# Declaring operations in different banks of one three-bank PSUM tile independent

## The chip, the cores and the metric

The kernel runs on one core of a Trainium2 chip. The metric is the device time of one execution in microseconds. Engines are named as in the profile: PE is TensorE (PEld its weight loads), DVE is VectorE, ACT is ScalarE, POOL is GpSimd, and SP is SyncE, whose queue starts most DMAs.

## The reference

Two layers in a row, all in float32. The first is attention that keeps, per query, the 32 largest scores; the second mixes channels of its output, with each row's predecessor mixed in.

```python
# q, k, v: (8, 8, 576, 64); d_model 512, d_ff 1024
scores = 1/sqrt(64) * q @ k.T
kth = the 32nd largest score of each row
attn = softmax(where(scores >= kth, scores, -1e9))
x = (attn @ v), heads laid side by side: (8, 576, 512)

x_prev = x shifted down by one row (a zero row first)
xk = mu_k * x + (1 - mu_k) * x_prev
xr = mu_r * x + (1 - mu_r) * x_prev
k = maximum(xk @ w_k, 0)
out = sigmoid(xr @ w_r) * ((k * k) @ w_v)
```

## The kernel before, in words

**Tiles of work.** Attention goes by visits: one batch, one pair of heads, and half of the query rows. A visit has four or five tiles of 128 x 576 scores. Tiles 0 to 7 of a head pair come in twos: tile i (even) belongs to the one head and tile i+1 to the other. Tile 8 holds the last 64 rows of both heads. For a pair of tiles the steps are these, with their engine and the line that the profile shows:

- *score* (PE, L890): two matmuls of 64 x 512, one for each head, one into bank 0 and one into bank 2 of the PSUM tile `ps`; the profile counts four, as a float32 matmul is done in two passes here. For tile 8 it is *score8* (L875, L877).
- *sliver* (PE, L885): the last 64 keys of both heads, into bank 1.
- *keep* (ACT, L895), twice: copies 576 scores to `sc`. For the first head they are columns 0 to 575 of `ps` (banks 0 and 1), for the second columns 960 to 1535 (banks 1 and 2).
- DVE, ACT and POOL then find the 32 largest (`cand` L900, `top` L902 and L923, `sg` L920 and L922), ACT takes exponentials (`se`, L928), and DVE masks them into `E` (L931).
- *turn* (PE, L937) transposes the first 512 columns of `E`, and ACT copies them to `et` (L939).
- *turnl* (PE, L946) transposes the last 64 columns of both heads into columns 832 to 959 of `ps` (bank 1), and ACT copies them to `el` (L948).
- *weigh* (PE, L969 and L971): the sums over values, from `et`, `el` and `v`, into columns 576 to 831 of `ps` (bank 1). It is in bank 1 like the data that `el` is copied from, so it follows that copy.
- *place* (DVE, L1005 for two pairs, L1008 for a single one): multiplies the sums by the inverse row sums and writes them to `xT`.

The second layer runs in chunks of 256 rows on `rot` tiles, which are separate PSUM tiles; its matmuls are L607 to L609. The weights are split into two parts at the start (L1174 to L1191).

**Order.** All operations are entered in a graph (`plan.op`) with a cost, a key and the buffers that they read and write. `Plan.run` then works out, engine by engine, an order with planned start times. In this plan a PSUM buffer has a list of banks, and an operation waits for other engines' operations in the same banks only. The operations are then issued in the planned order, and the program is built with that order as it stands (`tc.manual_schedule()`).

**Waits.** The kernel writes no semaphores. The framework that builds the program adds them, from the tiles that instructions share. `ps` is a single tile of three banks for it, and the planner's buffers are slices of it:

```python
a = pp.tile([128, 3 * 512], F32, name="ps")
made["psA"], made["psB"], made["sl"] = ([a[:, :512]], [(0,)], False), ([a[:, 1024:]], [(2,)], False), ([a], [(1,)], False)
made["sums0"], made["sums1"] = ([a[:, 576:704]], [(1,)], False), ([a[:, 704:832]], [(1,)], False)
made["last"] = [a[:, 832:960]], [(1,)], False
```

The second part of each entry is the planner's list of banks. Score has `psA` and `psB`, so banks 0 and 2. Sliver, turnl, `el`, weigh and place have bank 1. Keep has 0 and 1, or 1 and 2. Score8 has 0 and 1.

Of the kernel before, what the change touches and what calls it, by code (L numbers as in the profile page):

```python
# [13 lines left out]
AF = mybir.ActivationFunctionType  # L14
# [3 lines left out]
B, H, S, D = 8, 8, 576, 64  # L18
# [4 lines left out]
MAIN = 512  # L23
REST = S - MAIN
NKC = MAIN // 128
# [4 lines left out]
SCALE = 1.0 / math.sqrt(D)  # L30
BELOW = 1.0 - 2.0 ** -24
# [12 lines left out]
           w=13.895, wabs=-2.072, wclamp=0.971, wshift=-11.985, wsign=1.043, wexp=-1.834, wfine=-0.159, whi=3.263, wmul=9.248, wsub=-9.325, wlo=1.928,  # L44
# [16 lines left out]
LAST, JOINT, PEAT = "last", True, 112  # L61
LWAT, LWSTEP = 1.027, 1.455
LAG0, LAG1 = 10.828, 1.959
WPE = 12
MORE = dict(xh=2, xl=2, et=3, top=3, el=1)


class Buf:
    __slots__ = ("kind", "turn", "slot", "left", "users", "wrote", "read")
# [29 lines left out]


class Op:
    __slots__ = ("lane", "cost", "lat", "f", "base", "key", "pace", "mode", "bufs", "deps", "need", "then", "at", "end", "name", "n")


class Clock:
# [213 lines left out]
def planned(graph):  # L319
    return graph().run()[0]  # L320
# [3 lines left out]
def topk_attention_channel_mix(ctx: ExitStack, tc: tile.TileContext, q, k, v, mu_k, mu_r, w_k, w_v, w_r, out):  # L324
    nc = tc.nc
# [5 lines left out]
    ident = consts.tile([128, 128], F32, name="ident")  # L331
# [3 lines left out]
    ranks_i = consts.tile([128, 9], I32, name="ranks_i")  # L335
# [439 lines left out]
    def attend(plan, visits, X, pair_sums):  # L775
# [8 lines left out]
        for p, (b, hp, part) in enumerate(visits):  # L784
            P = Env()
# [71 lines left out]
            for i in part:  # L857
                n = at0 + i - P.first
                T = Env()
                T.i, T.P = i, P  # L860
                j, u = i % 2, i // 2 % 2
                if i % 4 == 0 or i == P.first:
                    U = Env()
# [3 lines left out]
                if i % 2 == 0:  # L867
                    E, el = buf("E"), buf("el")
                T.sc, T.cand, T.top = buf("sc"), buf("cand"), buf("top")
                if i == 8:  # L870
                    ps, sl = [buf("psA")], buf("sl")

                    def score8(P=P, ps=ps, sl=sl):
                        qd = P.kd.t[:, 128:]
                        nc.tensor.matmul(ps[0].t, lhsT=qd, rhs=P.K.t, start=True, stop=True)  # L875
                        for h in range(2):
                            nc.tensor.matmul(sl.t[:, MAIN:S], lhsT=qd, rhs=P.kd.t[:, h * 64:(h + 1) * 64], start=h == 0, stop=h == 1)  # L877
                    plan.op(PE_, "score8", n, 1190, 1380, score8, reads=[P.K, P.kd], writes=[*ps, sl], mode="Z")
                elif j == 0:
                    ps, sl = [buf("psA"), buf("psB")], buf("sl")  # L880
                    c = (i - P.first) // 2

                    def sliver(P=P, sl=sl, c=c):
                        to = sl.t[:, 512:1408].rearrange("p (h x) -> p h x", h=2)[:, :, :64]
                        nc.tensor.matmul(to, lhsT=P.qs.t[:, c * 128:(c + 1) * 128], rhs=P.kd.t[:, :128].rearrange("p (h x) -> p h x", h=2), start=True, stop=True)  # L885

                    def score(P=P, ps=ps, c=c):
                        for h in range(2):
                            w = slice(h * 64, (h + 1) * 64)
                            nc.tensor.matmul(ps[h].t, lhsT=P.qs.t[w, c * 128:(c + 1) * 128], rhs=P.K.t[w], start=True, stop=True)  # L890
                    plan.op(PE_, "score", n, 965, 1155, score, reads=[P.K, P.qs], writes=ps, mode="S")
                    plan.op(PE_, "sliver", n, 230, 420, sliver, reads=[P.kd, P.qs], writes=[sl], mode="T")

                def keep(T=T, x=ps[j] if i < 8 else ps[0], sl=sl, o=960 if j else 0):
                    nc.scalar.activation(T.sc.t, sl.t[:, o:o + S], AF.Copy)  # L895
                plan.op(ACT, "keep", n, 530, 648, keep, reads=[ps[j] if i < 8 else ps[0], sl], writes=[T.sc])
                for c in range(NCH):
                    w = CUTS[c + 1] - CUTS[c]
# [42 lines left out]
                if i % 2 or i == 8:  # L941
                    es = [T] if i == 8 else [tiles[i - 1], T]
                    pl = buf(LAST)

                    def turn_l(E=E, pl=pl, o=448 if i == 8 else 512):
                        nc.tensor.transpose(pl.t[:, :128], E.t[:, o:o + 128], ident)  # L946
                    plan.op(PE_, "turnl", n, 109, 300, turn_l, reads=[(E, jj) for jj in range(len(es))], writes=[pl, (el, "held")], mode="T")
                    plan.op(ACT, "el", n, 157, 285, lambda el=el, pl=pl: nc.scalar.activation(el.t, pl.t[:, :128], AF.Copy), reads=[pl], writes=[el])  # L948
                    u = (i - U.i) // 2
                    if u == 0:  # L950
                        U.pa = [buf(x) for x in ("sums0", "sums1")[:(U.w + 1) // 2]]

                    def weigh(U=U, P=P, es=es, el=el, u=u, i=i):
                        hs = [slice(j * 64, (j + 1) * 64) for j in range(2)]
                        if i < 8:
                            pa = U.pa[u].t
                            vs = [P.v.t[:, j] for j in range(2)]
                            vr = P.vr.t
                            ms = [[t.et.t[:, c * 128:(c + 1) * 128] for t in es] for c in range(NKC)]
                            ls = [el.t] * 2  # L960
                        else:
                            pa = U.pa[0].t[:, :64]
                            vs = [P.v.t[:, j] for j in range(2)]
                            vr = P.vr8.t
                            ms = [[es[0].et.t[:, c * 128 + j * 64:c * 128 + (j + 1) * 64] for j in range(2)] for c in range(NKC)]
                            ls = [el.t[:, h] for h in hs]
                        for c in range(NKC):
                            for j in range(2):
                                nc.tensor.matmul(pa[hs[j]], lhsT=vs[j][:, c, :], rhs=ms[c][j], start=(c == 0), stop=False)  # L969
                        for j in range(2):  # L970
                            nc.tensor.matmul(pa[hs[j]], lhsT=vr[:, j], rhs=ls[j], start=False, stop=True)  # L971
                    cost = 1140 if i < 8 else 629
                    plan.op(PE_, "weigh", n, cost, cost + 197, weigh, reads=[t.et for t in es] + [el] + [P.v, P.vr if i < 8 else P.vr8], writes=[U.pa[u]], mode="W")
                if i % 4 == 3 or i == part[-1]:
                    U.ri, pr = buf("ri"), buf("rot")
                    w, m = U.w, (U.w + 1) // 2
# [22 lines left out]
                    cost = 206 if i == 8 else 50 + 107 * m  # L999
                    plan.op(ACT, "ri", n, cost, cost + 117, out_ri, reads=[pr], writes=[U.ri])  # L1000

                    def place(U=U, x=xT[b], hp=hp, i=i, m=m):
                        to = x.t[:, hp, 1 + U.i * 64:1 + min(S, U.i * 64 + m * 128)]
                        if m == 2:
                            nc.vector.tensor_mul(to.rearrange("p (u q) -> p u q", u=2), pair_sums, U.ri.t.rearrange("p (u q) -> p u q", u=2))  # L1005
                        else:
                            n = 64 if i == 8 else 128
                            nc.vector.tensor_mul(to, U.pa[0].t[:, :n], U.ri.t[:, :n])  # L1008
                    cost = 130 if i == 8 else 64 + 136 * m
                    plan.op(DVE, "place", n, cost, cost + 90, place, reads=[*U.pa, U.ri], writes=[(xT[b], (hp, U.i // 2 + u)) for u in range(m)], after=X.late if b == 1 else ())  # L1010
                    for u in range(m):
# [1 line left out]
            if hp == HP - 1:  # L1013
                o = slice(part[0], part[-1] + 1)
# [181 lines left out]
    def pipeline(stack):  # L1196
        one = stack.enter_context(tc.tile_pool(name="one", bufs=1))
# [8 lines left out]
        made = {}  # L1206
# [14 lines left out]
        c = pp.tile([128, 2 * 512], F32, name="se")  # L1221
# [4 lines left out]
        pair_sums = a[:, 576:832].rearrange("p (u q) -> p u q", u=2)  # L1226
# [7 lines left out]
        def graph():  # L1234
            plan = Plan()
            for name, (tiles, banks, free) in made.items():
                plan.kind(name, len(tiles), banks, free)
                plan.kinds[name].tiles = tiles
            X = Env()
            X.ranks, X.least, X.mu = plan.buf("ranks"), plan.buf("least"), plan.buf("wmu")  # L1240
            def consts_in():
                nc.vector.tensor_copy(X.ranks.t[:, :9], ranks_i)
                if JOINT:
                    nc.vector.memset(X.ranks.t[:, 9:10], -SCALE)
                    nc.vector.memset(X.ranks.t[:, 10:11], BELOW)
            plan.op("DVE", "ranks", -9, 250, 350, consts_in, writes=[X.ranks])
            plan.op("SP", "mu", 1.0, 1100, 2900, load_mu, writes=[X.mu])
            plan.op("DVE", "nmu", 3.0, 80, 183, lambda: nc.vector.tensor_scalar(nmu, mu, -1.0, 1.0, op0=OP.mult, op1=OP.add), writes=[X.mu])
            weights(plan, X)
            mixes(plan, *attend(plan, VISITS, X, pair_sums), X)  # L1250
            return plan

        for o in planned(graph):
            o.f()

    with ExitStack() as stack:
        stack.enter_context(tc.manual_schedule())
# [12 lines left out]
    with tc.If(again > 0):  # L1270
        with tc.For_i(0, B, 1) as b, ExitStack() as stack:
# [8 lines left out]
            for hp in range(HP):  # L1280
                P = Env()
                P.hp = hp
                prep_all(g, P, lambda x: x[bass.ds(b, 1)].rearrange("o h s d -> (o h) s d"), hp, L)
                for i in range(9):
                    T = Tile_()
# [51 lines left out]
```

## Time and profile before

| | |
|---|---|
| median of 3 runs | 1324.69 us (1323.78 to 1325.32) |
| profiled execution, its own time | 1327.52 us |
| its span, from the first instruction to the last | 1325.7 us |
| PE busy | 1237.7 us (93%) |
| DVE busy | 1152.2 us (87%) |
| ACT busy | 1133.4 us (85%) |
| POOL busy | 985.9 us (74%) |
| mean granted PE clock | 0.988 |

The busy times are sums over a run whose first 60 us load and split weights and whose last 130 us have the second layer alone, so a share in the middle is higher than here. In lists of groups, "idle before" is the time that an engine sat idle just ahead of these instructions, with the instruction that ended the wait. Matmuls overlap by some 0.06 us, and their ends are modelled.

### The profile page before, as it was taken

The page shows a single profiled execution, that of the slowest core. Times are in us where ns is not written, and L with a number is a line of the kernel's source. Part 1 is how long each engine was busy: PE and PEld are TensorE (multiplying, and loading weights), DVE is VectorE, ACT ScalarE, POOL GpSimd, SP SyncE. Part 2 cuts the span into 40 slices and gives each one's busy share as a digit, 9 for nine tenths or more (in the row PEclk, how much of TensorE's full clock was granted, in tenths as well). Part 3 has the DMA queues.
Part 4 walks back from the last instruction along what each step waited for, and adds up shares of the span by engine and source line. Part 5 has one row for each costly group of instructions (what it writes and reads, how often), then busy time and mean ns, then how long its engine had stood idle before and what let it go on. Part 6 is the DMA issues. An engine that isn't in the chain of part 4 may idle for free.

```text
span 1325.7 us, 31110 instructions
## 1 busy us (share of the span) xinstructions
PE 1237.7 (93%) x9349; PEld 940.2 (71%) x9349; DVE 1152.2 (87%) x6228; ACT 1133.4 (85%) x2491; POOL 985.9 (74%) x885
## 2 busy tenths in 40 slices
PE   5877899999999999999999999999999999999996
PEld 2434667777677776777777777787777777777885
DVE  6999999999999998999999999999898999997211
ACT  5897899999998998899999999998989899988441
POOL 2457997878678685877779687786878788778682
PEclk9997999999999999999999999999999999999998
DMA  7143212221221212122221222212221222221100
GB/s 204 39 108 95 55 43 63 47 62 24 55 64 45 57 34 66 35 62 47 62 47 34 54 55 54 51 37 63 46 62 31 58 47 61 45 54 40 40 24 15
DMA packets 218593, 72.51 MB, mean 55 GB/s; under 512 B 211248, under 2 KB 211248, under 8 KB 218416
## 3 DMA queue, kind: packets, MB, share of 16 engines
q1 hardware_dynamic: 217872, 70.31, 21.6%
q8 instruction: 76, 1.25, 0.4%
q14 instruction: 101, 0.83, 0.2%
q10 hardware_dynamic: 544, 0.13, 0.0%
HBM read 60.95 MB, written 9.44 MB: 53 GB/s over the span
## 4 chain that ended last, share of the span: by engine, by line
PE 57%; ACT 20%; DVE 14%; POOL 3%; issue 3%; DMA 1%; SPq 1%; ACTq 0%; DVEq 0%; POOLq 0%
PE rot L607 9%; PE rot L609 8%; PE rot L608 8%; PE ps L890 8%; PE ps L969 7%; PE rot L937 6%; ACT sg L920 4%; ACT sc L895 4%; DVE cand L900 3%; ACT et L939 3%; ACT se L928 3%; DVE E L931 2%; PE ps L885 2%; DVE top L923 2%; PE rot L833 2%
## 5 line engine op out<-in xcount | busy, mean ns | idle before, releaser
L922 POOL TENSOR_TENSOR sg<-sc,sg 128x576 f32<-128x576 f32 x288 | 408.4, 1421 | 191.5 <-ACT sg L920 189.7
L900 DVE MAX8 cand<-sc 128x8 f32<-128x82 f32 (+1 forms) x2016 | 377.2, 231 | 23.7 <-ACT sc L895 21.8
L920 ACT ACTIVATE sg<-sc,seen 128x576 f32<-128x576 f32 x288 | 225.4, 783 | 14.2 <-DVE seen L912 12.7
L931 DVE SCALAR_TENSOR_TENSOR E<-sc,seen,se 128x576 f32<-128x576 f32 x288 | 231.0, 802 | 0.8 <-PE ps L946 0.2
L923 DVE MAX8 top<-sg 128x8 f32<-128x576 f32 x288 | 215.9, 750 | 11.6 <-POOL sg L922 10.6
L928 ACT ACTIVATE se<-sc,seen 128x576 f32<-128x576 f32 x288 | 216.8, 753 | 8.1 <-DVE E L931 6.3
L895 ACT ACTIVATE sc<-ps 128x576 f32<-128x576 f32 x288 | 186.5, 654 | 28.4 <-DVE E L931 10.2
L937 PE MATMUL rot<-ident,E 128*128 128x128 f32 x1152 | 180.9, 281 | 15.7 <-DVE E L931 7.2
L969 PEld LDWEIGHTS ps<-et,v 128*64 128x64 f32 x2560 | 130.9, 138 | 77.1 <-ACT el L948 46.7
L969 PE MATMUL ps<-et,v 128*64 128x128 f32 (+1 forms) x2560 | 169.5, 271 | 15.9 <-ACT el L948 13.7
L902 DVE MAX8 top<-cand 128x8 f32<-128x56 f32 x864 | 179.1, 208 | 3.7
L607 PE MATMUL rot<-xh,wk 128*128 128x256 f32 (+2 forms) x608 | 180.6, 297 | 1.3 <-ACT ri L998 0.5
L939 ACT ACTIVATE et<-rot 128x512 f32<-128x512 f32 x288 | 173.3, 603 | 7.5 <-PE rot L937 7.2
L937 PEld LDWEIGHTS rot<-ident,E 128*128 128x128 f32 x1152 | 130.0, 141 | 68.6 <-issue 11.4
L608 PE MATMUL rot<-xl,wk 128*128 128x256 f32 (+2 forms) x608 | 170.1, 280 | 0.9 <-POOL xl L1092 0.9
L609 PE MATMUL rot<-xh,wk 128*128 128x256 f32 (+2 forms) x608 | 169.9, 279 | 0.0
L890 PE MATMUL ps<-K,qs 64*128 64x512 f32 x512 | 148.3, 657 | 2.2 <-ACT el L948 1.5
L607 PE MATMUL rot<-wv,hh 128*128 128x512 f32 (+1 forms) x296 | 127.2, 430 | 0.4 <-ACT qs L838 0.3
L607 PEld LDWEIGHTS rot<-xh,wk 128*128 128x128 f32 x608 | 116.4, 191 | 5.2 <-ACT qs L838 1.5
L609 PE MATMUL rot<-wv,hl 128*128 128x512 f32 (+1 forms) x296 | 116.9, 395 | 0.0
L608 PEld LDWEIGHTS rot<-xl,wk 128*128 128x128 f32 x608 | 115.9, 191 | 1.1 <-POOL xl L1092 1.1
L608 PE MATMUL rot<-wv,hh 128*128 128x512 f32 (+1 forms) x296 | 115.9, 392 | 0.0
(113 smaller groups left out, 2834.6 us busy)
## 6 DMA issues: line engine op xcount, KB each, us to landing
kn<-in_k SPq DMA_DIRECT2D x136, 128.0 KB, 2.5
v<-in_v SPq DMA_DIRECT2D x136, 128.0 KB, 2.5
out<-eb SPq DMA_DIRECT2D x35, 256.0 KB, 2.2
qn<-in_q SPq DMA_DIRECT2D x126, 64.0 KB, 2.2
stage<-in_moe_w_k SPq DMA_DIRECT2D x8, 512.0 KB, 6.3
xT<-in_moe_w_v SPq DMA_DIRECT2D x8, 512.0 KB, 3.6
tl<-in_k SPq DMA_DIRECT2D x136, 16.0 KB, 2.0
vr_in<-in_v SPq DMA_DIRECT2D x128, 16.0 KB, 2.1
```

The costliest lines, as they stand in the source:

```text
L607: nc.tensor.matmul(ps, lhsT=sh, rhs=mh, start=first, stop=False)
L608: nc.tensor.matmul(ps, lhsT=sh, rhs=ml, start=False, stop=False)
L609: nc.tensor.matmul(ps, lhsT=sl, rhs=mh, start=False, stop=last)
L890: nc.tensor.matmul(ps[h].t, lhsT=P.qs.t[w, c * 128:(c + 1) * 128], rhs=P.K.t[w], start=True, stop=True)
L900: lambda T=T, c=c: nc.vector.max(T.cand.t[:, 8 * c:8 * c + 8], T.sc.t[:, CUTS[c]:CUTS[c + 1]]), reads=[T.sc], writes=[(T.cand, c)])
L920: lambda T=T, sn=sn: nc.scalar.activation(T.side.t, T.sc.t, AF.Sign, bias=sn(T, 1), scale=-BELOW, accum_out=T.top.t[:, TOPK:TOPK + 1]),
L922: plan.op(POOL, "below", n, 1375, 1430, lambda T=T: nc.gpsimd.tensor_mul(T.side.t, T.sc.t, T.side.t), reads=[T.sc], writes=[T.side])
L923: plan.op(DVE, "eighth", n, 660, 754, lambda T=T: nc.vector.max(T.top.t[:, 24:32], T.side.t), reads=[T.side], writes=[(T.top, 3)])
L928: plan.op(ACT, "exps", n, 667, 754, lambda T=T, pe=pe, sn=sn: nc.scalar.activation(pe.t, T.sc.t, AF.Exp, bias=sn(T, 0), scale=SCALE), read ...
L931: lambda T=T, U=U, pe=pe, sn=sn: nc.vector.scalar_tensor_tensor(T.e(), T.sc.t, sn(T, 2), pe.t, op0=OP.is_ge, op1=OP.mult, accum_out=U.rs.t ...
L937: nc.tensor.transpose(pt.t[:, c * 128:(c + 1) * 128], E.t[:, o + c * 128:o + (c + 1) * 128], ident)
L969: nc.tensor.matmul(pa[hs[j]], lhsT=vs[j][:, c, :], rhs=ms[c][j], start=(c == 0), stop=False)
```

## The change

The functions that issue operations now return their instructions. After each operation is issued, in the planned order, its banks are looked up. If all of them are among 0, 1 and 2, which are those of `ps`, the operation is compared with the last 16 such operations. Where the other one is of another engine, has no bank in common with it and no buffer slot in common with it, every instruction of the one is declared free of a dependency on every instruction of the other. Order, tiles and operations are the same.

```diff
+LOOK = 16
...
 class Op:
-    __slots__ = (..., "name", "n")
+    __slots__ = (..., "name", "n", "made")
...
                     def score(P=P, ps=ps, c=c):
-                        for h in range(2):
-                            w = slice(h * 64, (h + 1) * 64)
-                            nc.tensor.matmul(ps[h].t, lhsT=P.qs.t[w, c * 128:(c + 1) * 128], rhs=P.K.t[w], start=True, stop=True)
+                        ws = [slice(h * 64, (h + 1) * 64) for h in range(2)]
+                        return [nc.tensor.matmul(ps[h].t, lhsT=P.qs.t[w, c * 128:(c + 1) * 128], rhs=P.K.t[w], start=True, stop=True) for h, w in enumerate(ws)]
...
+        past = []
         for o in planned(graph):
-            o.f()
+            got = o.f()
+            banks = {k for b in o.bufs for k in b.kind.banks[b.slot]}
+            if banks and banks <= {0, 1, 2}:
+                o.made = [x.ins for x in (got if isinstance(got, list) else [got])]
+                slots = {(b.kind, b.slot) for b in o.bufs}
+                for p, bs, ss in past:
+                    if p.lane != o.lane and not bs & banks and not ss & slots:
+                        for x in o.made:
+                            for y in p.made:
+                                tc.declare_no_dep(x, y, reason="other banks of one tile")
+                past = [*past, (o, banks, slots)][-LOOK:]
```

The other functions that write or read `ps` (score8, sliver, keep, turn_l, weigh, place) get the same `return`.

More of the change, by code (lines that the diff above doesn't have):

```diff
@@ L101 @@
 class Op:
-    __slots__ = ("lane", "cost", "lat", "f", "base", "key", "pace", "mode", "bufs", "deps", "need", "then", "at", "end", "name", "n")
+    __slots__ = ("lane", "cost", "lat", "f", "base", "key", "pace", "mode", "bufs", "deps", "need", "then", "at", "end", "name", "n", "made")
 class Clock:
@@ L874, in score8 @@
                         qd = P.kd.t[:, 128:]
-                        nc.tensor.matmul(ps[0].t, lhsT=qd, rhs=P.K.t, start=True, stop=True)
-                        for h in range(2):
-                            nc.tensor.matmul(sl.t[:, MAIN:S], lhsT=qd, rhs=P.kd.t[:, h * 64:(h + 1) * 64], start=h == 0, stop=h == 1)
+                        return [nc.tensor.matmul(ps[0].t, lhsT=qd, rhs=P.K.t, start=True, stop=True),
+                                *[nc.tensor.matmul(sl.t[:, MAIN:S], lhsT=qd, rhs=P.kd.t[:, h * 64:(h + 1) * 64], start=h == 0, stop=h == 1) for h in range(2)]]
                     plan.op(PE_, "score8", n, 1190, 1380, score8, reads=[P.K, P.kd], writes=[*ps, sl], mode="Z")
@@ L884, in sliver @@
                         to = sl.t[:, 512:1408].rearrange("p (h x) -> p h x", h=2)[:, :, :64]
-                        nc.tensor.matmul(to, lhsT=P.qs.t[:, c * 128:(c + 1) * 128], rhs=P.kd.t[:, :128].rearrange("p (h x) -> p h x", h=2), start=True, stop=True)
+                        return nc.tensor.matmul(to, lhsT=P.qs.t[:, c * 128:(c + 1) * 128], rhs=P.kd.t[:, :128].rearrange("p (h x) -> p h x", h=2), start=True, stop=True)
                     def score(P=P, ps=ps, c=c):
-                        for h in range(2):
-                            w = slice(h * 64, (h + 1) * 64)
-                            nc.tensor.matmul(ps[h].t, lhsT=P.qs.t[w, c * 128:(c + 1) * 128], rhs=P.K.t[w], start=True, stop=True)
+                        ws = [slice(h * 64, (h + 1) * 64) for h in range(2)]
+                        return [nc.tensor.matmul(ps[h].t, lhsT=P.qs.t[w, c * 128:(c + 1) * 128], rhs=P.K.t[w], start=True, stop=True) for h, w in enumerate(ws)]
                     plan.op(PE_, "score", n, 965, 1155, score, reads=[P.K, P.qs], writes=ps, mode="S")
@@ L894, in keep @@
                 def keep(T=T, x=ps[j] if i < 8 else ps[0], sl=sl, o=960 if j else 0):
-                    nc.scalar.activation(T.sc.t, sl.t[:, o:o + S], AF.Copy)
+                    return nc.scalar.activation(T.sc.t, sl.t[:, o:o + S], AF.Copy)
                 plan.op(ACT, "keep", n, 530, 648, keep, reads=[ps[j] if i < 8 else ps[0], sl], writes=[T.sc])
@@ L945, in turn_l @@
                     def turn_l(E=E, pl=pl, o=448 if i == 8 else 512):
-                        nc.tensor.transpose(pl.t[:, :128], E.t[:, o:o + 128], ident)
+                        return nc.tensor.transpose(pl.t[:, :128], E.t[:, o:o + 128], ident)
                     plan.op(PE_, "turnl", n, 109, 300, turn_l, reads=[(E, jj) for jj in range(len(es))], writes=[pl, (el, "held")], mode="T")
@@ L966, in weigh @@
                             ls = [el.t[:, h] for h in hs]
[L967 to L971, printed above, removed]
+                        return [*[nc.tensor.matmul(pa[hs[j]], lhsT=vs[j][:, c, :], rhs=ms[c][j], start=(c == 0), stop=False) for c in range(NKC) for j in range(2)],
+                                *[nc.tensor.matmul(pa[hs[j]], lhsT=vr[:, j], rhs=ls[j], start=False, stop=True) for j in range(2)]]
                     cost = 1140 if i < 8 else 629
@@ L1004, in place @@
                         if m == 2:
[L1005 to L1008, printed above, removed]
+                            return nc.vector.tensor_mul(to.rearrange("p (u q) -> p u q", u=2), pair_sums, U.ri.t.rearrange("p (u q) -> p u q", u=2))
+                        n = 64 if i == 8 else 128
+                        return nc.vector.tensor_mul(to, U.pa[0].t[:, :n], U.ri.t[:, :n])
                     cost = 130 if i == 8 else 64 + 136 * m
@@ L1241, in consts_in @@
             def consts_in():
[L1242 to L1245, printed above, removed]
+                return [nc.vector.tensor_copy(X.ranks.t[:, :9], ranks_i), nc.vector.memset(X.ranks.t[:, 9:10], -SCALE), nc.vector.memset(X.ranks.t[:, 10:11], BELOW)]
             plan.op("DVE", "ranks", -9, 250, 350, consts_in, writes=[X.ranks])
```

## The prediction

> **What bounds the kernel now.** I read the page first: span, busy times and the chain that ended last.
> ```profile
> span 1325.7 us, 31110 instructions
> PE 1237.7 (93%) x9349; PEld 940.2 (71%) x9349; DVE 1152.2 (87%) x6228; ACT 1133.4 (85%) x2491; POOL 985.9 (74%) x885
> PE 57%; ACT 20%; DVE 14%; POOL 3%; issue 3%; DMA 1%; SPq 1%; ACTq 0%; DVEq 0%; POOLq 0%
> ```
> No engine is the bound by itself: TensorE (PE) carries 57% of the chain, and the chain crosses over to ScalarE (ACT) and VectorE (DVE) for another third. So I split the body of the run, 60 to 1195 us, with the view of busy time by stretch (columns: stretch, its length, busy time of PE, PEld, DVE, ACT, POOL, then granted clock, DMA).
> ```profile
> 60.00:400.00 340.00, 304.81 (x2322) 224.56 (x2321) 324.86 (x1742) 307.58 (x674) 263.18 (x231) 0.97 0.24 61
> 400.00:700.00 300.00, 288.32 (x2253) 219.76 (x2252) 279.79 (x1570) 270.60 (x603) 228.16 (x202) 1.00 0.21 50
> 700.00:1195.00 495.00, 484.91 (x3814) 377.04 (x3812) 463.17 (x2574) 451.96 (x1001) 389.61 (x346) 1.00 0.21 51
> ```
> Up to 400 us DVE is the tight engine: 15.1 us idle against 35.2 on PE. From 400 us on it is PE: 11.7 and 10.1 us idle, against 20.2 and 31.8 on DVE.
>
> Next I asked for the waits of PE over the whole run, and for the copy `el` (L948), which the list puts first. In the answer for L948, the lines before the "who waited for it" pair say what ended ACT's idle time ahead of it (us, times); the last two say who sat idle for it.
> ```profile
> PE ps L969 <- ACT el L948: 13.7, 36, 0.4
> PE ps L885 <- ACT sc L895: 7.4, 16, 1.0
> PE rot L937 <- DVE E L931: 7.2, 6, 3.2
> ```
> ```profile
> L948 ACT ACTIVATE el<-ps x160: 253/277/326, 37.6 to 1239.3; 128x128 f32<-128x128 f32 x160
>   PE ps L890: 37.2, 51
>   PE ps L946: 7.4, 12
>   PEld ps L969: 46.7, 49
>   PE ps L969: 13.7, 36
> ```
> `el` copies what the transpose L946 wrote in bank 1. Yet in 51 of its 160 runs ACT stood idle for it, 37.2 us in all, until the **score** matmuls L890 had ended, which write banks 0 and 2 and give `el` nothing. The transpose itself was the late one only 12 times. And PE's largest wait among those above is the weigh (L969) for `el`. The timeline shows one such place:
> ```profile
> 568.96 0.27 PE L946 MATMUL ps<-ident,E 128*128 128x128 f32 x1
> 569.15 0.59 ACT L939 ACTIVATE et<-rot 128x512 f32<-128x512 f32 x1
> 569.17 1.13 PE L890 MATMUL ps<-K,qs 64*128 64x512 f32 x4
> 570.34 0.28 ACT L948 ACTIVATE el<-ps 128x128 f32<-128x128 f32 x1 [0.61 <-PE ps L890]
> 570.67 1.09 PE L969 MATMUL ps<-et,v 128*64 128x128 f32 x16 [0.38 <-ACT el L948]
> ```
> The transpose ends at 569.23, ACT is free at 569.74, but `el` starts at 570.34, when the score ends (569.17 + 1.13 = 570.30). PE has nothing else in its order than the weigh, and idles 0.38 us. The order puts the score between transpose and weigh, where it would cover the copy; the wait undoes that. This is a wait for a neighbour in the same tile, and it is the one the change takes away.
>
> **The change part by part.**
>
> *What it leaves.* Every operation, its engine's order, its tiles and DMAs. Nothing is moved past any queue. In the planner's bank lists, the score holds banks 0 and 2; sliver, transpose, `el`, weigh and `place` hold 1; the copy `sc` (L895) holds 0 and 1, or 1 and 2; score8 holds 0 and 1. Pairs on two engines with no bank in common are then only score with `el`, and score with `place` (L1005, L1008), in both directions. Waits of the weigh for `el`, of the sliver for `sc` and so on stay, as bank 1 is common to them.
>
> *Score, then `el`.* Price of one stall on PE: in the rows above from the score's start to the weigh's, 570.67 - 569.17 = 1.50 us. Where nothing holds what follows the score, the timeline has
> ```profile
> 85.86 1.13 PE L890 MATMUL ps<-K,qs 64*128 64x512 f32 x4
> 86.92 1.13 PE L1189 MATMUL rot<-eb,ident 128*128 128x512 f32 x2
> ```
> so 1.06 us. A stall costs 0.44 us (the 0.38 us shown plus 0.06 of overlap). By stretch (60 to 400, 400 to 700, 700 to 1195) PE's waits are:
> ```profile
> PE ps L969 <- ACT el L948: 4.6, 12, 0.4
> PE ps L969 <- ACT el L948: 5.5, 14, 0.4
> PE ps L969 <- ACT el L948: 3.6, 10, 0.4
> ```
> 36 x 0.44 = 15.8 us: 5.3, 6.2 and 4.4. Can `el` really go 0.44 us earlier? ACT's mean idle time ahead of it is 37.2 / 51 = 0.73 us and the score's 1.06 us lies between transpose and weigh, so mostly yes. Going through the timeline, 33 of the 36 stalls stand behind an `el` that waited for the score; the first, one of the shortest, and the last of them are
> ```profile
> 103.44 0.28 ACT L948 ACTIVATE el<-ps 128x128 f32<-128x128 f32 x1 [1.67 <-PE ps L890]
> 387.72 0.28 ACT L948 ACTIVATE el<-ps 128x128 f32<-128x128 f32 x1 [0.20 <-PE ps L890]
> 1181.43 0.28 ACT L948 ACTIVATE el<-ps 128x128 f32<-128x128 f32 x1 [0.60 <-PE ps L890]
> ```
> In four of the 33, as in the second line, ACT had less than 0.44 us to give, 0.8 us short in all. With 3 x 0.44 for the three others I take off 2 us: **13.8 us** of PE time. The copy will now run while PE writes the neighbouring banks; its longest run is 326 ns against a median of 277, so if that made every such copy slow it would be 51 x 0.05 = 2.5 us on ACT, and nothing on PE while the score's 1.06 us covers it. I take 0. Next in line there is `et` (L939), which the weigh needs too: where it follows `el` on ACT it moves forward with it, and the score covers it.
>
> *`el` or `place`, then score.* For L890 the waits are
> ```profile
> PE ps L890 <- ACT el L948: 1.5, 5, 0.4
> ```
> and, in the answer for L890, where weight loads count too,
> ```profile
> DVE xT L1005: 1.3, 2
> ```
> On PE about 1.5 + 0.6 us, taking half of the second: **2 us**, nearly all after 700 us.
>
> *Score, then `place`.* On DVE:
> ```profile
> DVE xT L1005 <- PE ps L890: 6.6, 9, 1.0
> DVE xT L1008 <- PE ps L890: 3.8, 6, 0.8
> ```
> **10.4 us** of DVE idle time. What would hold `place` next is the weigh before the score, about 1 us earlier. Only up to 400 us is DVE the tight engine, so a small part counts.
>
> *Semaphores.* `el` now vouches for less, so `sc` may have to wait for the score by itself. The row of such separate waits at `sc`:
> ```profile
> L895 ACTq EVENT_SEMAPHORE  x181: 17/17/1016, 27.2 to 1193.9; - x181
> ```
> 17 ns for 51 places is 0.9 us on ACT if all become new, and as much saved if they go at `el` instead. I take 0: both are hidden in ACT's own idle time, 9% of the stretches above.
>
> *What reaches the end.* Since the order is fixed and no duration changes, an earlier start can only be passed on or be absorbed by another wait. How much is kept I choose by stretch:
> - 60 to 400 us, DVE tight: of PE's 5.3 us I keep 0.4, so 2.1, and of DVE's and ACT's idle 1.5.
> - 400 to 700 us: `el` is 5.5 of PE's 11.7 us of idle, and PE runs at 96.1% there while it runs at 98.0% after 700 us with the other engines about as loaded. So PE can be that full: I keep 0.85 of 6.2, so 5.3.
> - 700 to 1195 us: 0.85 of 4.4 + 2, so 5.4.
>
> That is 14.3 us; less 0.85 of the 2 us taken off above, **12.6 us**. Bounds from the rows: from below, if only the chain's PE share is kept, 0.57 x 15.8 = 9.0. From above, with every idle microsecond counted by its engine's share of the chain, 9.0 + 0.20 x 37.2 + 0.14 x 10.4 = 17.9. The value lies between these.
>
> The profiled execution took 1327.5 us around its span of 1325.7; less 12.6 it is 1314.9. The median of the three runs stands 2.8 us lower, at 1324.69: **1312 us**.
>
> **The rivals.**
>
> *Absorbed by DVE and ACT.* The gain on PE turns into waits for `sc` (7.4 us now) and for `E` (7.2 us now). For it: DVE is 93 to 96% busy, ACT about 91%. Against it: PE at 98.0% after 700 us. If a fifth of 15.8 is kept plus 1.5 on DVE: 4.7 us, so 1320.
>
> *More is kept.* ACT's 37.2 us also start `et`, `sc` and the mask's inputs earlier, and other waits of PE shrink with them. With twice the ACT term of the upper bound: 17.9 + 7.4 = 25.3 less, 1299.
>
> *Nothing happens.* The declaration comes after the instructions are made; if the wait is already drawn, or the pair is taken in the other direction, the same waits remain: 1324.7. For it: the profile does not show how waits are drawn. Against it: no data passes from score to `el`, so their common tile is all that this wait can come from, and that is what is declared away.
>
> *Slower, by the clock.* PE's clock falls to half after slack windows:
> ```profile
> 97.98:101.39 3.41, 1.56 (x12) 1.06 (x11) 3.41 (x14) 3.18 (x8) 1.90 (x2) 1.00 0.23 51
> 101.39:104.81 3.42, 3.05 (x13) 1.27 (x14) 3.42 (x17) 1.75 (x5) 1.99 (x2) 0.50 0.33 104
> 497.34:500.75 3.41, 2.44 (x14) 2.06 (x14) 2.93 (x20) 3.41 (x7) 1.36 (x2) 1.00 0.60 134
> ```
> A window with PE 46% busy is followed by half clock; at 72% (the slackest after 140 us) it is not. A window of 3.4 us at half clock costs PE 1.7 us. If PE, now ahead of DVE, bunches its waits, more windows could fall under that mark. To end slower than 1327.3 it must cost 12.6 + 2.6 = 15.2 us, nine such windows; that is the point from which it decides, and with twelve the time is 1332. Against it: after 140 us none does, and the change takes idle time out of PE's windows. The Trainium skill, "TensorE: Matmul & The Clock Gate", in its Part 1 on the clock gate, has the clock fall only after an idle window of about 3.4 us. By that rule this rival is void and the sum stays; the trace is stricter, since the first window above was 46% busy and its longest idle stretch was this:
> ```profile
> 99.49 0.44 PE L846 MATMUL rot<-ident,tl 128*128 128x128 f32 x2 [1.41 <-ACT wr L1191]
> ```
> I go by the trace and leave the rival a small chance.
>
> **How the numbers follow.** Forecast, 1306 to 1317: 0.60. More kept, under 1306: 0.12. Absorbed, 1317 to 1322.7: 0.16. Nothing happens: 0.07. Slower: 0.05. Within 0.2% (1322.0 to 1327.3) is about what a measurement of this kernel can't tell from no change. Faster: 0.60 + 0.12 + 0.14 = 0.86, since a little of "absorbed" falls within the bound; same 0.02 + 0.07 = 0.09; slower 0.05. The range leaves out the 0.07, the 0.05 and the outer part of "more": 1303 to 1320.5.
>
> **What would show it.** In the profile after, `el`'s idle time until L890 goes from 37.2 us to nearly nothing and its wait for L946 grows a little; the weigh's wait for `el` goes from 13.7 us to under 3; the same for L1005 and L1008 behind L890. PE's busy share in 400 to 700 us rises to about 98%; its waits for `sc` and `E` grow by a few us. Instruction counts of the engines stay, and so does each order. It is wrong if `el` still waits for L890, or if the waits for `sc` and `E` grow by as much as the others fell, or if the granted clock is below 1.00 anywhere after 140 us.

## The result and the profile after

The changed kernel takes 1282.72 us (median of 4 runs, 1281.8 to 1286.54) against 1325.01 us for the kernel before beside it: ratio 0.9681, 95% interval 0.9653 to 0.971. It is 42.3 us faster. The forecast was 12.6 us, and the range ended at 1303: the direction was right, the size wrong by more than a factor of three.

The page after, with the same three lines as before (line numbers of the changed file differ by a few: score is L889, sliver L885, `cand` L899, `sc` L894, `E` L930, *turn* L936, `et` L938, *turnl* L945, `el` L947, the weigh L966, `place` L1001 and L1003):
```profile
span 1281.5 us, 31120 instructions
PE 1218.4 (95%) x9349; PEld 935.8 (73%) x9349; DVE 1146.5 (89%) x6228; ACT 1131.4 (88%) x2491; POOL 985.8 (77%) x885
PE 46%; DVE 25%; ACT 18%; POOL 4%; issue 3%; DMA 2%; SPq 1%; DVEq 0%; ACTq 0%; POOLq 0%
```
The counts of instructions on the engines are the same. The answer for `el`, with the lines on what ended ACT's idle time ahead of it, and on who sat idle for it:
```profile
L947 ACT ACTIVATE el<-ps x160: 251/278/373, 35.8 to 1194.8; 128x128 f32<-128x128 f32 x160
L947 ACTq EVENT_SEMAPHORE  x32: 17/17/17, 88.4 to 1194.7; - x32
  PE ps L945: 8.4, 13
...
  PEld ps L966: 16.5, 24
  PE ps L966: 0.5, 1
```
The 37.2 us of waiting for the score are gone, at all of the 51 places, and PE's stall at the weigh went from 13.7 us to 0.5. At `place` too, no line names the score any more. The timeline of the place shown before (568.96 us there) now reads:
```profile
544.53 0.27 PE L945 MATMUL ps<-ident,E 128*128 128x128 f32 x1
544.58 0.59 ACT L938 ACTIVATE et<-rot 128x512 f32<-128x512 f32 x1
544.73 1.13 PE L889 MATMUL ps<-K,qs 64*128 64x512 f32 x4
545.06 0.28 ACT L947 ACTIVATE el<-ps 128x128 f32<-128x128 f32 x1
545.79 1.09 PE L966 MATMUL ps<-et,v 128*64 128x128 f32 x16
```
`el` runs under the score, and the weigh follows 1.06 us after the score's start, the step of an unhindered score, in place of 1.50.

For the busy times by stretch (columns as before) I moved the borders 60, 400, 700 and 1195 us to where the same work stands after, by the lead that ACT and DVE have there (1.6, 15.9, 30.8 and 44.1 us):
```profile
58.40:384.10 325.70, 297.82 (x2304) 221.84 (x2304) 321.41 (x1737) 305.22 (x670) 261.83 (x230) 0.98 0.25 63
384.10:669.20 285.10, 283.10 (x2275) 219.62 (x2272) 279.02 (x1573) 272.05 (x606) 228.68 (x204) 1.00 0.22 53
669.20:1150.90 481.70, 480.06 (x3815) 377.01 (x3814) 462.21 (x2577) 451.08 (x1002) 390.69 (x346) 1.00 0.22 52
```
The stretches are 14.3, 14.9 and 13.3 us shorter. PE's idle time fell from 35.2, 11.7 and 10.1 us to 27.9, 2.0 and 1.6, that is by 25.5 us. The other 17.1 us were in PE's busy time, 1078.05 us before and 1060.98 after for nearly the same matmuls (8389 and 8394 records). The busy time of DVE and ACT fell by 5.2 and 1.8 us. In the first stretch the granted clock was 0.97 before and 0.98 after, so part of PE's 7.0 us there can be the clock. In the other two it was 1.00 both times, and 10.1 us went all the same. So "98% busy" before was not a PE near its end. The reading that fits is that part of its stalls were written down as busy.

### The profile page after: what moved, and what is told of

The parts are those of the page before. It is cut to its first block, busy times and chain, and to the rows that moved or that the text cites. A ratio compares the mean times of both kernels' runs of the same rounds, so it can differ in the third digit from the quotient of the medians.

```text
span 1281.5 us, 31120 instructions
## 1 busy us (share of the span) xinstructions
PE 1218.4 (95%) x9349; PEld 935.8 (73%) x9349; DVE 1146.5 (89%) x6228; ACT 1131.4 (88%) x2491; POOL 985.8 (77%) x885
## 4 chain that ended last, share of the span: by engine, by line
PE 46%; DVE 25%; ACT 18%; POOL 4%; issue 3%; DMA 2%; SPq 1%; DVEq 0%; ACTq 0%; POOLq 0%
PE rot L608 7%; PE rot L610 7%; PE rot L609 7%; DVE cand L899 7%; PE ps L966 6%; PE rot L936 5%; DVE E L930 5%; PE ps L889 5%; DVE top L922 4%; ACT sc L894 4%; ACT sg L919 3%; ACT se L927 3%; ACT et L938 2%; DVE top L901 2%; DVE cand L904 2%
## 5 line engine op out<-in xcount | busy, mean ns | idle before, releaser
L899 DVE MAX8 cand<-sc 128x8 f32<-128x82 f32 (+1 forms) x2016 | 377.0, 231 | 18.2 <-ACT sc L894 16.3
L919 ACT ACTIVATE sg<-sc,seen 128x576 f32<-128x576 f32 x288 | 226.1, 785 | 13.8 <-DVE seen L911 12.2
L930 DVE SCALAR_TENSOR_TENSOR E<-sc,seen,se 128x576 f32<-128x576 f32 x288 | 231.0, 802 | 0.8 <-issue 0.2
L894 ACT ACTIVATE sc<-ps 128x576 f32<-128x576 f32 x288 | 186.9, 656 | 22.0 <-DVE E L930 8.2
L936 PE MATMUL rot<-ident,E 128*128 128x128 f32 x1152 | 179.6, 279 | 13.7 <-DVE E L930 7.2
L938 ACT ACTIVATE et<-rot 128x512 f32<-128x512 f32 x288 | 174.1, 606 | 7.4 <-PE rot L936 7.1
L936 PEld LDWEIGHTS rot<-ident,E 128*128 128x128 f32 x1152 | 129.9, 141 | 63.9 <-ACT sg L919 7.3
L966 PEld LDWEIGHTS ps<-et,v 128*64 128x64 f32 x2560 | 128.5, 137 | 57.0 <-ACT el L947 16.5
L966 PE MATMUL ps<-et,v 128*64 128x128 f32 (+1 forms) x2560 | 164.6, 270 | 1.5 <-DVE seen L911 0.5
L889 PE MATMUL ps<-K,qs 64*128 64x512 f32 x512 | 147.4, 653 | 0.0
L608 PE MATMUL rot<-wv,hh 128*128 128x512 f32 (+1 forms) x296 | 127.0, 429 | 0.3 <-ACT qs L839 0.3
L904 DVE MATCH_REPLACE8 cand<-top,cand 128x56 f32<-128x56 f32 x576 | 115.8, 201 | 0.2 <-issue 0.2
```

Of the source, the lines that this page charges most:

```text
L608: nc.tensor.matmul(ps, lhsT=sh, rhs=mh, start=first, stop=False)
L894: return nc.scalar.activation(T.sc.t, sl.t[:, o:o + S], AF.Copy)
L899: lambda T=T, c=c: nc.vector.max(T.cand.t[:, 8 * c:8 * c + 8], T.sc.t[:, CUTS[c]:CUTS[c + 1]]), reads=[T.sc], writes=[(T.cand, c)])
L919: lambda T=T, sn=sn: nc.scalar.activation(T.side.t, T.sc.t, AF.Sign, bias=sn(T, 1), scale=-BELOW, accum_out=T.top.t[:, TOPK:TOPK + 1]),
L930: lambda T=T, U=U, pe=pe, sn=sn: nc.vector.scalar_tensor_tensor(T.e(), T.sc.t, sn(T, 2), pe.t, op0=OP.is_ge, op1=OP.mult, accum_out=U.rs.t ...
L936: nc.tensor.transpose(pt.t[:, c * 128:(c + 1) * 128], E.t[:, o + c * 128:o + (c + 1) * 128], ident)
```

## The experiments

Each kernel was timed in the same session as the kernel before; microseconds gained or lost are worked out from the ratios, times 1325. "Above" means above the changed kernel, by the difference of the two ratios.

**Which pair carries the gain?** Four kernels restrict the pairs that are declared, each by one more condition in the same line:

```diff
-                    if p.lane != o.lane and not bs & banks and not ss & slots:
+                    if ... and "el" in (o.name, p.name):       # e1
+                    if ... and "place" in (o.name, p.name):    # e2
+                    if ... and o.name == "el":                 # e3
+                    if ... and o.lane == "PE":                 # e4
```

Only score and `el`, both directions.

> Only pairs of score and `el` are declared independent, in both directions; score and `place` still wait for each other. Theory A (ACT's idle time ahead of `el` and PE's stall behind it carry the gain, and ACT's lead then shortens other waits of PE): 36 to 41 of the 42 us come, so 1284 to 1289 us, and L966's wait for `el` on PE is under 2 us. Theory B (`place` on DVE, which is 94 to 99% busy, carries a good part): 20 to 30 us come, 1295 to 1305. Theory C (the two only work together, the chain crosses over to whichever is left): under 25 us here and under 5 us from the other pair alone.

Measured: 1292.31 us, ratio 0.9758 (0.974 to 0.9775), 32 us of the 42. PE's wait for `el` at the weigh is 0.5 us, as A said, but the gain lies between A's band (36 to 41) and B's (20 to 30). C falls.

Only score and `place`.

> Only pairs of score and `place` are declared independent; score and `el` still wait for each other. Theory A: 1 to 6 us faster than before, about 1320 us. Theory B: 12 to 20 us faster, 1305 to 1313. Theory C: under 5 us, and together with the run for `el` alone over 10 us short of the sum of the whole change.

Measured: 1317.05 us, ratio 0.9941 (0.9924 to 0.9957), 8 us: between A and B again. The two pairs add up, 32 + 8 = 40 against 42, so none of the three theories has the size right. In this kernel `el` stands where it stood before, as its answer shows (idle time of ACT ahead of `el`, then who waited for `el`):
```profile
  PE ps L889: 37.4, 51
  PE ps L966: 14.1, 37
```
So freeing score and `place` is worth 8 us, where DVE had waited 10.4 us, with PE's stall behind `el` untouched.

Only one direction: `el` not behind an earlier score.

> Of the four directions only one is declared: an `el` does not wait for the score issued before it. Score still waits for an earlier `el` or `place`, and `place` for an earlier score. Theory A: 33 to 40 us faster than before, 1285 to 1292 us. Theory B: 18 to 27 us. If the waits of score itself matter more than the 2 us summed for them, this run falls short of the one for `el` in both directions by more than 4 us.

Measured: 1295.62 us, ratio 0.9773 (0.9757 to 0.9789), 30 us, again between the bands of A and B. That is 2 us less than e1, within the intervals. Of `el`'s waits the one for the transpose is left, and the weigh's for `el` is gone:
```profile
  PE ps L945: 10.1, 15
  PE ps L966: 0.4, 1
```
One direction of one pair, 51 waits, makes most of the result.

Only the directions in which the score comes later.

> Only the directions in which score is the later one are declared: score does not wait for an earlier `el` or `place`; both still wait for an earlier score. Theory A and the sum in the prediction: 1 to 4 us faster than before, about 1322 us, with PE's waits of L889 for `el` gone. If PE's stalls ahead of score are worth more than their own length (as the stalls at the weigh seem to be): 5 us or more.

Measured: 1324.42 us, ratio 0.9988 (0.9978 to 0.9998), 1.6 us, by the interval 0.3 to 2.9. The 2 us of the prediction's sum fit.

**What does a microsecond cost, by engine?** The 30 us of e3 stand against 13.8 us of stalls on PE and 37.2 us of idle time on ACT, at the same places. To part the two I gave time back to one engine at a time in the changed kernel, with work of no use and without any new wait for the score.

```diff
+            if o.name == "el" and at in EL:        # f1, f3: the 51 places
+                nc.scalar.activation(spare, wide, AF.Copy)
...
+                        if nth["score"] - 1 in SC:     # f2, f3: the 37 scores
+                            made.append(nc.tensor.matmul(ps[1].t[:, :416], lhsT=P.qs.t[ws[1], c * 128:(c + 1) * 128], rhs=P.K.t[ws[1]][:, :416], start=True, stop=True))
...
+            if o.name == "place" and at in PL:     # f4: the 15 places
+                nc.vector.tensor_mul(spare, wide, wide)
```

> The changed kernel, with a copy of 128 x 640 on ACT (about 0.73 us, of no use to the result) right behind `el`, at the 51 places where `el` had waited for the score: 37 us of ACT time given back, while `el` itself and the weigh are not held up. Theory 'ACT' (ACT's time at these places is on the path, for its lead starts `et`, `sc` and the exponentials): 22 to 34 us above the changed kernel, 1305 to 1317 us. Rival 'PE' (the gain is PE's 15.8 us of stalls and their echo; ACT had slack): under 10 us, 1283 to 1293.

Measured: 1305.42 us, ratio 0.9846 (0.9824 to 0.9868), 22 us above the changed kernel.
```profile
L1254 ACT ACTIVATE spare<-ident x51: 724/750/924, 36.0 to 1160.1; 128x640 f32<-128x640 f32 x51
PE 1234.2 (95%) x9349; PEld 939.1 (72%) x9349; DVE 1148.5 (88%) x6228; ACT 1159.8 (89%) x2542; POOL 986.7 (76%) x885
```
ACT's busy time rose by 28.4 us (successive copies overlap a little), so a microsecond on ACT cost 0.77. The granted clock is not behind it: the four runs, at 0.981 to 0.987, lie within 0.6 us of each other. PE had nothing added, yet its busy time rose by 15.8 us. Part of that is the clock, 0.83 between 60 and 140 us against 0.91 in the changed kernel. From 140 to 1140 us it was 1.00 in both, and there PE was busy 981.50 us for 7779 matmul records against 990.57 for 7915, 0.8% more for each, some 8 us in all: again what stalls written down as busy would give. The rival "PE" with its under 10 us falls.

How ACT's time reaches another engine shows in DVE's wait for `sc`, in the kernel before, in the changed one and in this one:
```profile
DVE cand L900 <- ACT sc L895: 21.8, 30, 3.2
DVE cand L899 <- ACT sc L894: 16.3, 18, 3.6
DVE cand L899 <- ACT sc L894: 21.8, 30, 2.9
```
The filler brought this wait back to what it was, though `el` didn't wait for the score.

> The changed kernel, with 416 of 512 columns of the score's second matmul done once more (about 0.43 us, same result) at the 37 scores behind which the weigh had stalled: 16 us of PE time given back, ahead of the weigh, while ACT's `el` is not held up. Theory 'PE': 14 to 30 us above the changed kernel, 1297 to 1313 us, the more the longer its echo. Theory 'ACT': PE is 99% busy from 400 us on and lets nothing through free, so 10 to 16 us, 1293 to 1299.

Measured: 1303.83 us, ratio 0.9834 (0.9808 to 0.9861), 20 us above. The filler was longer than planned (score is L890 and the weigh L970 in this file):
```profile
556.56 1.13 PE L890 MATMUL ps<-K,qs 64*128 64x512 f32 x4
557.53 0.86 PE L892 MATMUL ps<-K,qs 64*128 64x416 f32 x2
558.31 1.09 PE L970 MATMUL ps<-et,v 128*64 128x128 f32 x16
```
From score to weigh it is 1.75 us in place of 1.06, so 0.69 us at each of 37 places, 25.5 us in all: 0.80 for a microsecond of PE. (PE's busy time rose by 21.3 us only; by that count it is 0.95.) The 20 us lie in the band of theory "PE" only because of that, so this run parts nothing by itself.

> Both fillers, 37 us on ACT and 16 us on PE at the places where both had idled: what the wait of `el` for the score took, but without the wait. If the loss was one of two engines' time, about as much as that wait cost, 30 to 38 us above the changed kernel, 1313 to 1321 us; if the two add up without overlap, the sum of the two fillers' runs.

Measured: 1314.05 us, ratio 0.9904 (0.9879 to 0.9928), 29.5 us above. This is just under the band, and far from the 42 us that the two fillers cost in sum: of the time lost on ACT and on PE at the same places, a good part is lost only once. That it comes so near to what the wait of `el` cost (30 us in e3) is partly chance, as the fillers took about 28 us on ACT and 25.5 on PE, and the wait had taken 37.2 and 13.8.

> The changed kernel, with a multiplication of 128 x 640 on DVE (about 0.7 us, of no use) ahead of `place` at the 15 places where it had waited for the score: 10.4 us of DVE time given back. If DVE's time is on the path nearly in full (as 8.3 us for the pair of `place` alone says): 7 to 10 us above the changed kernel, 1290 to 1293 us. If the gain of that pair came otherwise (score not held up by `place`, PE): under 4 us.

Measured: 1299.22 us, ratio 0.9802 (0.9778 to 0.9826), 16 us above, more than expected; but this filler too was longer than planned:
```profile
L1253 DVE TENSOR_TENSOR spare<-ident x15: 816/1416/1965, 115.8 to 1125.4; 128x640 f32<-128x640 f32 x15
PE 1222.3 (94%) x9349; PEld 933.5 (72%) x9349; DVE 1165.1 (90%) x6243; ACT 1131.9 (87%) x2491; POOL 993.0 (77%) x885
```
DVE's busy time rose by 18.6 us, so 0.86 for a microsecond. POOL's rose too, by 7.2 us, so the price may not be DVE's alone.

**Are those places special?** The same kinds of filler, away from `el`, score and `place`; and a smaller one in the old place.

```diff
+            if o.lane == "ACT":                    # g1
+                nth += 1
+                if nth % 43 == 0:
+                    nc.scalar.activation(spare, wide, AF.Copy)
...
+            if o.name == "turn":                   # g2
+                nth += 1
+                if nth % 8 == 0:
+                    o.f()
...
+            if o.name == "eighth":                 # g3
+                nth += 1
+                if nth % 10 == 0:
+                    o.f()
...
-        wide = ident[:, None, :].to_broadcast([128, 5, 128])
+        wide = ident[:, None, :].to_broadcast([128, 2, 128])   # g4, else as f1
```

> The changed kernel, with the same copy of 128 x 640 on ACT (0.63 us from its start to that of the next) behind every 43rd ACT operation of the run, 51 places that have nothing to do with `el` or score. Theory G (ACT, DVE and PE are all so full that a microsecond of any of them, anywhere, costs about 0.8): 20 to 27 us above the changed kernel, 1303 to 1310 us. Rival S (the path runs through the places of the removed waits; elsewhere ACT has slack): 0 to 12 us, 1283 to 1295.

Measured: 1303.39 us, ratio 0.9834 (0.9818 to 0.9851), 20 us above.
```profile
L1253 ACT ACTIVATE spare<-ident x48: 721/738/806, 39.5 to 1246.3; 128x640 f32<-128x640 f32 x48
PE 1233.0 (95%) x9349; PEld 940.4 (72%) x9349; DVE 1149.7 (88%) x6228; ACT 1157.7 (89%) x2539; POOL 986.0 (76%) x885
```
The trace has 48 of the fillers and 26.3 us more on ACT: 0.77 for a microsecond, the same as at `el`. For ACT theory G holds, at the lower edge of its band, and the rival S falls.

> The changed kernel, with the four transposes of every 8th `turn` (L936) done twice, 36 places, 0.44 us each: 16 us of PE time away from score and weigh. Theory G: 12 to 16 us above the changed kernel, 1295 to 1299 us. Rival S: under 7 us.

Measured: 1292.31 us, ratio 0.9754 (0.9737 to 0.977), 10 us above for 15.5 us more of PE busy time: 0.62. It lies between the two theories' bands, nearer to G.

> The changed kernel, with the search of 8 in 576 (`top` from `sg`, L922, about 0.66 us) done twice in every 10th tile, 28 places: 18.5 us of DVE time away from `place`. Theory G: 13 to 18 us above the changed kernel, 1296 to 1301 us. Rival S: under 8 us.

Measured: 1301.01 us, ratio 0.9821 (0.9805 to 0.9838), 18.5 us above for 18.0 us more of DVE busy time: 1.0, just over G's band. POOL's busy time stayed here (986.0 us).

> The filler behind `el` at the 51 places again, but 128 x 256, about 0.3 us instead of 0.63: 15 us of ACT time in place of 32. If there is no slack at these places, the cost falls in proportion, from 21 to about 10 us above the changed kernel (1293). If each place has some 0.15 us of slack that a filler must use up first, it falls to 5 to 7 us (1288 to 1290).

Measured: 1292.17 us, ratio 0.975 (0.9734 to 0.9766), 9 us above for 13.1 us more on ACT: 0.70, so near in proportion. There is hardly any slack that a filler uses up first.

Each of these differences from the changed kernel is uncertain by about 5 us, as both ratios have intervals of some 0.003 to either side. The changed kernel's share of this error is common to all of them. So the two prices of PE, 0.62 and 0.80, can't be told apart here, nor the two of DVE, 0.86 and 1.0. But g2 and g3 were timed together, and 9 us lie between them for 2.5 us more of filler: there a microsecond of DVE did cost more than one of PE. And none of the three prices of ACT is near the 0.20, none of DVE near the 0.14, that the prediction's upper bound had given them.

## Why the prediction was wrong

**The wait and its place: right.** Only score with `el` and score with `place` were freed. All 51 waits of `el` for the score are gone, `el` now starts under the score, and the next wait in line there is the one named, for the transpose (7.4 to 8.4 us).

**The terms: right in size.** PE's stall at the weigh, 0.44 us a piece: the rows after show 1.06 us in place of 1.50. Score behind `el` or `place`, 2 us: e4 measured 1.6. DVE's idle time at `place`, 10.4 us: no such line is left. Semaphores, 0: separate waits at `sc` went from 181 to 190 and at `el` from 35 to 32, of 17 ns each as a rule. The copy beside a running score, 0: `el` took 278 ns in the median after and 277 before. One count was off without effect: five of the 33 stalls, not four, had less than 0.44 us to win, 0.9 us in all.

**What reaches the end: wrong, and this is the step that failed.** It had two faults. First, it took PE's stalls as the main term and kept 0.4 to 0.85 of them, while the 37.2 us of ACT and the 10.4 us of DVE got 1.5 us together. Measured, score with `place` alone gives 8 us with 10.4 us of idle time taken from DVE, and a microsecond of ACT costs 0.70 to 0.77, at `el` and spread over the run. 0.77 x 37.2 = 28.6 us, where e3 gave 30. PE's 13.8 us are not to be added in full: f3 shows that the two overlap. With 0.86 x 10.4 = 8.9 us for DVE and 1.6 us from e4 the sum is 39 us, near the 42.3.

Second, the upper bound of 17.9 us valued an engine's idle time by its share of the chain. That share tells through which engine one path of one execution ran. It is no price: ACT had 20% of the chain, and its microseconds cost 0.70 to 0.77. When ACT is late, `et`, `sc` and the exponentials come late, then PE and DVE wait for them, as DVE's wait for `sc` in f1 shows.

A better measure that the profile of before did hold is the waiters' own idle time, 37.2 + 10.4 + 2 = 49.6 us. The result is 85% of it. That was found afterwards, on one kernel, and no run shows that it is a bound. In the stretches PE, DVE and ACT were each 91 to 95% busy (1078, 1068 and 1030 of 1135 us). That none had much time to make up what it lost is the likely reason, and was not tested by itself.

**The rivals.** "Absorbed" did not happen: PE's wait of 7.4 us for `sc` did not grow but fell, and the one for `E` stayed:
```profile
PE rot L936 <- DVE E L930: 7.2, 4, 4.2
PE ps L885 <- ACT sc L894: 5.0, 10, 1.2
```
"More is kept" named the mechanism that happened, ACT's lead shortening other waits, but with twice the ACT term of the bound above it still had 25.3 us and a chance of 0.12. "Nothing happens" and "slower" did not occur: the waits are gone, and the granted clock in the two later stretches is 1.00, as before.

**The PE share that could be reached.** I took 98.0% after 700 us as what PE can be filled to. After the change it is 283.10 / 285.1 = 99.3% and 480.06 / 481.7 = 99.7%, with 17 us less busy time for the same work.

**What stays open.** Why a microsecond of DVE in g3 cost more than one of PE in g2 was not followed up. How PE's busy time can hide a stall is read from sums of busy time alone; no run takes it apart.

## What to carry to other kernels

When the row of an engine that waits names work which gives it no data, look for a shared tile: independence that a planner assumes by bank has to reach the waits too. Value such a wait by the idle time of the engine that waits. In this kernel, where three engines are over 90% busy through the body of the run, a microsecond was worth 0.6 to 1.0, whichever of them the chain happened to run through. Where another engine idles behind the same wait, don't add its time in full. To learn the price, add a useless operation of known length to one engine and see what the end does.

## What the runs showed of the hardware

A lone matmul on 64 rows cost far more than half of a pair: the score's two took 1.06 us together from start to next start, but one more of 416 columns added 0.69 us. Part of the reason can be read off the rows, where the pair's four passes overlap (0.59 us the shortest, 0.69 in the median, 1.13 us for all four) and the two passes of the lone one lie mostly behind each other (0.51 us each, 0.86 us for both).

The multiplication of 128 x 640 on DVE took 0.82 to 1.97 us with both inputs repeated from a 128 x 128 tile, and POOL's busy time rose by 7.2 us in that run. Whether the two held each other up was not tried.
